# ScalarE takes over row statistics, the issue of two kinds of DMA, and a new order of the work

## The chip, the cores and the metric

The kernel runs on one core of a Trainium2 chip. A core has five engines, each with its own in-order stream of instructions: TensorE (PE, matrix multiply), VectorE (DVE), ScalarE (ACT), GpSimd (POOL) and SyncE (SP), which here does nothing but issue DMA transfers. They meet only through semaphores. An instruction that waits holds back everything behind it on its engine. The time is the device time of one execution, in microseconds (us). Before the change it was 1371.41 us, the median of three runs that lay between 1362.38 and 1377.51.

## The reference

Four transformer-like layers, A B A B, over 2048 tokens of width 512, with 32 heads of 16. Each layer normalizes its rows, projects to q, k and v, attends, projects back and adds to the residual. All of it is float32.

```python
x = x + _A_ref(_layernorm(x), A_wqkv, A_wo)
x = x + _B_ref(_layernorm(x), B_wqkv, B_wo)
x = x + _A_ref(_layernorm(x), A_wqkv, A_wo)
x = x + _B_ref(_layernorm(x), B_wqkv, B_wo)

def _layernorm(x, eps=1e-5):
    m, v = mean(x), var(x)              # over the 512 of a row
    return (x - m) / sqrt(v + eps)
# A: each token attends to itself and 7 earlier tokens, 2 apart
# B: each token attends to the 256 latest tokens, itself included
#    p = softmax(where(mask, q @ k.T * 16**-0.5, -1e9)); o = p @ v
```

## The kernel before, in words

**Tiling.** The tokens are cut into 8 chunks of 256. One B layer follows an A layer on the same chunks, so the work is a row of 32 scopes: A0, B0, A1, B1 and so on to A15, B15 (two passes over 8 chunks). All scopes overlap in time as far as their data and buffers allow.

**Precision.** Matmul operands that must be exact are split into a high float16 part and a low one (`xh`, `xl`; `eh`, `el`; `oh`, `ol`), and three products (high by high, high by low, low by high) are summed.

**Norm** (`norm`, L738). For each of the two halves of a chunk, DVE takes mean and variance (`stats`, L749 to L751), POOL makes the reciprocal standard deviation (`rstd`, L753 to L757), ACT writes the normalized rows (`xnorm`, L769) and their float16 high part (L781), SP issues a DMA that turns the high part (`turn_h`, L775), POOL or DVE subtracts (`rest`, L772) and SP issues the DMA that turns the low part (`turn_l`, L778). The projections on PE (L802 to L804 transposed, L823 plain) read the turned parts.

**Layer A.** ACT copies q, k, v out of PSUM (L936, L938). DVE or POOL forms the products of q with shifted k (`prod`, L960) and adds pairs (`plus`, L967); PE sums them to scores (L974); a softmax over 8 follows; DVE weighs v (L1046), and POOL or DVE adds up (`total`, L1051 to L1055).

**Layer B.** ACT writes the high part of q and k (`high`, L1074), DVE the low part (`low`, L1077). SP issues the writes of both to DRAM (`put`, L1087; twelve per scope, eight of them of high parts) and reads them back stacked along the rows (`stack`, L1098). A first pass of scores on PE (`tri`, `full`, L1130) gives DVE the row maxima (L1153, L1154, L1173); `mturn` (L1181 to L1184) joins and transposes them, ACT and POOL split them (L1187 to L1191), and SP sends them through DRAM (L1197) into the stacked operand (L1202). A second pass of scores (L1224) has the maxima subtracted by the matmul itself; ACT takes the exponentials (L1234), POOL masks them (L1245), PE multiplies with v (L1259). The score tiles `sc` have two buffers, so the DVE's reading of one frees it for PE's next.

**End of a layer** (`finish`, L833). The result is split, projected by `wo` (L823), and `done` (L867 to L869, DVE) adds it to the residual rows; SP stores them (L876, L880) and loads rows for the next norm (L843, L907).

**The order.** Nothing is scheduled while the program is built or run. Every step is a task with an engine and a cost in us, and a table `ORDER` gives, for each scope and each task in turn, its place on its engine. A negative entry means that the task goes to its other engine (DVE in place of POOL, or the reverse). `Plan.order` then walks through the queues and emits the instructions; costs only decide how the engines' streams are interleaved in the text of the program, and every engine's own order is that of the table.

```python
t.place, t.alt = ORDER[self.scope][self.k] if self.scope in ORDER else len(self.tasks), alt
if t.place < 0:
    (t.eng, t.us), t.place = alt, -1 - t.place
```

The functions that the change touches, and what calls them, with the line numbers of the profile:

Of the kernel before, what the change touches and what calls it, by code (L numbers as in the profile page):

```python
# [11 lines left out]
F32 = mybir.dt.float32  # L12
I32 = mybir.dt.int32
I16 = mybir.dt.int16
AF = mybir.ActivationFunctionType
# [26 lines left out]
        2, 3, 4, 4, 6, 6, 9, 4, 12, 8, 13, 11, 14, 13, 2, 1, 1, 0, 0, 3, 2, 7, 3, 33, 7, 5, 9, 7, 5, 10, 8, 11, 15, 17, 9, 25, 12, 18, 15, 17, 14,  # L42
        14, 15, 9, 12, 29, 20, 16, 45, 23, 32, 30, 34, 29, 36,
    ],
    "pB": [
        27, 43, 18, 44, 91, 89, 50, 95, 53, 49, 59, -75, 50, 66, -78, 17, 40, 25, 31, 84, 83, 46, 90, 49, 70, 45, 46, -60, 48, 51, 18, 26, 41, 20,
        27, 96, 97, 54, 100, 56, 55, 56, -62, 52, 53, -61, 6, 26, 15, 25, 54, 59, 31, 63, 35, 128, 37, 47, 35, 70, 86, 66, 19, 25, 36, 62, 1, 29, 31,
        28, 30,
    ],
# [4 lines left out]
    ],  # L54
# [5 lines left out]
    ],  # L60
# [8 lines left out]
    ],  # L69
# [5 lines left out]
    ],  # L75
# [10 lines left out]
    ],  # L86
# [5 lines left out]
    ],  # L92
# [1323 lines left out]
```

## Time and profile before

| what | us |
|---|---|
| median of three runs | 1371.41 |
| profiled execution | 1373.37 |
| its span, first to last instruction | 1371.6 |
| TensorE busy in it | 1246.9 |
| VectorE busy | 1142.3 |
| GpSimd busy | 955.4 |
| ScalarE busy | 733.7 |

The clock granted to TensorE was 0.973 of full speed on average. In the rows of the profile, `L802` is line 802 of the kernel, PEld is TensorE's loading of weights, and SPq or ACTq is the issue of a DMA by SP or ACT. A name such as `stk<-re` says that `stk` is written from `re`. Issuing a DMA is not counted as busy, although the engine does nothing else meanwhile. Busy times, waits and durations are those of the profiled execution.

### The profile page before, as it was taken

Reading aid. Unit: us, or ns where it says so; the run is one execution under the profiler, and the core shown is the slowest. Engines: PE = TensorE matmul, PEld = TensorE weight load, DVE = VectorE, ACT = ScalarE, POOL = GpSimd, SP = SyncE. Lnnn points to the kernel's source line nnn. Section 1 sums busy time; section 2 is a strip of 40 time slices with the busy share of each in tenths; the row PEclk is TensorE's granted clock in tenths of the full one; section 3 lists DMA queues with packets and bytes.
Section 4 is the critical chain, followed back from the end, with each engine's and each line's share of the span. In section 5 each row is a group of like instructions: output and inputs, shape, how many; then the busy total and the mean of one; then the engine's idle time right before and its main releaser. Section 6 shows DMA issues by size and latency. Waiting matters only on the chain.

```text
span 1371.6 us, 47863 instructions
## 1 busy us (share of the span) xinstructions
PE 1246.9 (91%) x20752; PEld 847.8 (62%) x20752; DVE 1142.3 (83%) x1482; ACT 733.7 (53%) x1035; POOL 955.4 (70%) x1013
## 2 busy tenths in 40 slices
PE   6869999989998898999999999998998999998877
PEld 4546666657566665666667666766666666664544
DVE  5968978887887888789899999798987988988574
ACT  7543454646555464655556464555555566365544
POOL 4357678778686877877686768888678877666233
PEclk9989999999999999999999999999999999999989
DMA  8204243334434332444434444433444434234322
GB/s 279 60 16 137 60 126 90 121 84 121 82 78 129 94 112 69 115 110 106 119 90 124 106 115 108 99 108 78 136 100 111 93 97 118 54 96 112 97 73 64
DMA packets 172467, 140.17 MB, mean 102 GB/s; under 512 B 105184, under 2 KB 131296, under 8 KB 172256
## 3 DMA queue, kind: packets, MB, share of 16 engines
q1 hardware_dynamic: 172000, 136.85, 38.1%
q8 instruction: 162, 2.65, 0.8%
q14 instruction: 49, 0.40, 0.1%
q10 hardware_dynamic: 256, 0.26, 0.1%
HBM read 67.11 MB, written 43.48 MB: 81 GB/s over the span
## 4 chain that ended last, share of the span: by engine, by line
PE 20%; DVE 12%; DMA 7%; SPq 4%; issue 3%; ACT 2%; POOL 2%; ACTq 0%; DVEq 0%; POOLq 0%
PE av L1259 3%; PE po L823 3%; PE pq L802 3%; PE pq L803 2%; PE pq L804 2%; DVE st L1153 2%; DVE m L1154 2%; DVE pw L1046 2%; DVE m L1173 2%; PE st L1130 2%; DMA xl<-xn 1%; DMA stk<-re 1%; SPq L1098 1%; DMA os<-scr 1%; SPq L1314 1%
## 5 line engine op out<-in xcount | busy, mean ns | idle before, releaser
L960 POOL TENSOR_TENSOR pr<-kv,q 128x1024 f32<-128x1024 f32 x76 | 170.5, 2253 | 41.9 <-DVE pr L967 16.2
L1153 DVE COPY_PREDICATED st<-maskt,st 128x512 f32<-128x512 int16 x224 | 154.0, 687 | 50.1 <-PE st L1130 46.1
L1234 ACT ACTIVATE p_H<-sk_H,scales 128x1024 f32<-128x1024 f32 x128 | 142.4, 1113 | 93.8 <-PE sk_H L1224 82.3
L1234 ACT ACTIVATE p_F<-sk_F,scales 128x1024 f32<-128x1024 f32 (+1 forms) x128 | 135.6, 1060 | 102.8 <-PE sk_F L1224 97.5
L1245 POOL TENSOR_SCALAR_AFFINE_SELECT p_H<-p_H 128x1024 f32<-128x1024 f32 x128 | 143.0, 1118 | 50.5 <-ACT p_H L1234 50.2
L1245 POOL TENSOR_SCALAR_AFFINE_SELECT p_L<-p_L 128x1024 f32<-128x1024 f32 x112 | 125.7, 1125 | 59.6 <-ACT p_L L1234 59.3
L1046 DVE TENSOR_TENSOR pw<-pb,kv 128x1024 f32<-128x1024 f32 x128 | 151.0, 1211 | 17.6 <-PE pb L1033 16.1
L1173 DVE TENSOR_REDUCE m<-sf 128x8 f32<-128x1024 f32 x120 | 144.8, 1211 | 22.8 <-PE sf L1130 22.5
L1154 DVE TENSOR_REDUCE m<-st 128x4 f32<-128x512 f32 x224 | 154.7, 691 | 7.7
L1234 ACT ACTIVATE p_L<-sk_L,scales 128x1024 f32<-128x1024 f32 x112 | 124.0, 1113 | 67.1 <-PE sk_L L1224 64.2
L1130 PEld LDWEIGHTS <-stk 48*128 48x128 f16 x2880 | 90.3, 95 | 109.3 <-issue 69.6
L1224 PEld LDWEIGHTS <-stk 64*128 64x128 f16 x2880 | 90.8, 95 | 100.8 <-issue 60.1
L1053 POOL TENSOR_TENSOR pw<-pw 128x512 f32<-128x512 f32 x87 | 110.9, 1274 | 28.8 <-DVE pw L1046 27.7
L1130 PE MATMUL st<-stk,stk 48*128 48x128 f16 x1920 | 97.4, 220 | 22.9 <-DMA stk<-re 8.0
L967 POOL TENSOR_TENSOR pr<-pr,pr 128x1024 f32<-128x1024 f32 x31 | 73.0, 2356 | 26.0 <-DVE pr L960 25.6
L1259 PE MATMUL av<-p_H,v 128*32 128x128 f32 x2048 | 81.1, 276 | 0.8 <-POOL p_H L1245 0.8
L1051 DVE TENSOR_REDUCE o<-pw 128x128 f32<-128x1024 f32 x41 | 79.9, 1953 | 0.2
L1259 PE MATMUL av<-p_F,v 128*32 128x128 f32 x1920 | 78.9, 280 | 0.7 <-ACT p_F L1234 0.6
L803 PE MATMUL pq<-xl,wA1h 128*128 128x256 f16 x256 | 70.7, 276 | 6.6 <-DMA xl<-xn 6.6
L960 DVE TENSOR_TENSOR pr<-kv,q 128x1024 f32<-128x1024 f32 x52 | 72.6, 1411 | 4.7 <-POOL pr L967 4.0
L803 PE MATMUL pq<-xl,wB1h 128*128 128x256 f16 x256 | 70.5, 275 | 6.5 <-DMA xl<-xn 6.3
L823 PEld LDWEIGHTS <-oh 128*32 128x32 f16 x2048 | 49.2, 98 | 43.5 <-issue 5.6
(194 smaller groups left out, 3592.7 us busy)
## 6 DMA issues: line engine op xcount, KB each, us to landing
stk<-re SPq DMA_DIRECT2D x256, 96.0 KB
re<-eh SPq DMA_DIRECT2D x128, 128.0 KB
xm<-xr SPq DMA_DIRECT2D x32, 256.0 KB
re<-el SPq DMA_DIRECT2D x64, 128.0 KB
xr<-xm SPq DMA_DIRECT2D x16, 512.0 KB
oc<-os SPq DMA_DIRECT2D x120, 64.0 KB
os<-scr SPq DMA_DIRECT2D x15, 512.0 KB
x<-in_A_x_dram SPq DMA_DIRECT2D x8, 512.0 KB
```

Of the source, the lines that this page charges most:

```text
L803: nc.tensor.matmul(ps[mp].t[:, i], wh, xl, start=False, stop=False)
L960: E.tensor_mul(pr.t, window(kv[1].t, m, P * n, P), qb)
L1046: nc.vector.tensor_mul(pw.t, pb.t.unsqueeze(1).broadcast_to([P, 2, W, 64]), v)
L1053: E.tensor_add(t[:, :, 0:4], t[:, :, 0:4], t[:, :, 4:8])
L1130: nc.tensor.matmul(ps.t[:, par, at * P : (at + 1) * P], stk[hf, 0][r, col, qb * P : (qb + 1) * P], stk[hf, kt][r, col, kb * P : (kb + 1) * ...
L1153: nc.vector.copy_predicated(v[:, :, 0::2], maskt[:, 0:P].bitcast(I16).unsqueeze(1).unsqueeze(1).broadcast_to([P, 2, 2, P]), v[:, :, 1::2])
L1154: nc.vector.tensor_reduce(out=m[:, 0, :, us[0]], in_=v[:, :, 0::2], op=ALU.max, axis=AX.X)
L1173: nc.vector.tensor_reduce(out=o, in_=v, op=ALU.max, axis=AX.X)
L1224: nc.tensor.matmul(ps.t[:, par, at * P : (at + 1) * P], stk[hf, kt][r, col, kb * P : (kb + 1) * P], stk[hf, 0][r, col, qb * P : (qb + 1) * ...
L1234: nc.scalar.activation(o, i, AF.Exp, scale=scl["B", 1])
L1245: nc.gpsimd.affine_select(out=v, in_=v, pattern=[[0, 8], [-1 if kind == "L" else 1, P]], compare_op=ALU.is_gt if kind == "L" else ALU.is_g ...
L1259: nc.tensor.matmul(acc.t[32 * mm : 32 * mm + 32, hq, qb * P : (qb + 1) * P], v[:, 17 * (H * kb + h) : 17 * (H * kb + h) + 32], p[:, mm % 2 ...
```

## The change

1. **Row statistics.** `stats` on the DVE is gone. ACT computes the variance of each half by a pass with Square, bias minus the mean and a sum over the row. In A layers ACT also computes the sum of the row by a pass with Copy; in B layers that sum comes from `done` of the A layer before, which now also returns the sum of each row that it writes.
2. **DMA issue.** `turn_h` and the writes of the high parts of q and k are issued by ACT in place of SP. The low parts stay on SP.
3. **Maxima.** `mturn` joins the two sets of maxima by a reduction that also doubles them, and transposes into the tile `mt`.
4. **Order.** `ORDER` is a new table for all scopes, prologue included, with other choices between DVE and POOL; some of the planner's costs change, and its cost for a change of matmul form goes from 0.15 to 0.17.

The diff, without the 550 lines of the table:

```diff
-TURN = 0.15
+TURN = 0.17
...
-        mv = buf("psm", [P, 2, 2], F32, "mv", f"mv{l}_{c}")
+        sums = layers[l] == "A"
+        if sums:
+            mv = buf("psm", [P, 2, 2], F32, "mv", f"mv{l}_{c}")
+            vsm = [Val(mv), Val(mv)]
+        else:
+            mv, vsm = x_sum[c]
...
-        def stats(t):
-            nc.vector.bn_stats(b6[t].t, xb.t[:, t])
-            nc.vector.bn_aggr(mv.t[:, t], b6[t].t)
+        xns = [buf("pxn", [P, D], F32, "xn", f"xn{l}_{c}_{t}") for t in range(2)]
+        vxq = [Val(x) for x in xns]
+
+        def rowsum(t):
+            nc.scalar.activation(xns[t].t, xb.t[:, t], AF.Copy, accum_out=mv.t[:, 0, t : t + 1])
+
+        def rowvar(t):
+            nc.scalar.activation(xns[t].t, xb.t[:, t], AF.Square, bias=mv.t[:, 0, t : t + 1], scale=-float(D), accum_out=mv.t[:, 1, t : t + 1])
...
         for t in range(2):
-            plan.add("DVE", 0.82, lambda t=t: stats(t), r=[vx[t]], w=[vmv[t], Val(b6[t])])
-        plan.add("POOL", 2.3, rstd, r=vmv, w=[vrs])
+            if sums:
+                plan.add("ACT", 0.72, lambda f=rowsum, t=t: f(t), r=[vx[t]], w=[vsm[t], vxq[t]])
+            plan.add("ACT", 0.72, lambda f=rowvar, t=t: f(t), r=[vx[t], vsm[t]], w=[vsq[t], vxq[t]])
+        plan.add("POOL", 1.95, rstd, r=vsq, w=[vrs])
...
             def turn_h(t=t, hi=hi):
-                nc.sync.dma_start_transpose(xh.t[:, :, t * P : (t + 1) * P], hi.t)
+                nc.scalar.dma_start_transpose(xh.t[:, :, t * P : (t + 1) * P], hi.t)
...
-            plan.add("SP", 1.26, turn_h, r=[vhi], w=[vh], size=10)
+            plan.add("ACT", 1.26, turn_h, r=[vhi], w=[vh], size=10)
...
-            def done(t=t, ps=ps):
+            def done(t=t, ps=ps, mv=x_sum[c][0] if T == "A" else None):
                 xt = xb.t[:, t]
-                nc.vector.scalar_tensor_tensor(xt, ps.t, scl[T, 3], xt, op0=ALU.mult, op1=ALU.add)
+                kw = {"accum_out": mv.t[:, 0, t : t + 1]} if mv else {}
+                nc.vector.scalar_tensor_tensor(xt, ps.t, scl[T, 3], xt, op0=ALU.mult, op1=ALU.add, **kw)
...
-                        nc.sync.dma_start(re.t[z, :, :, par].rearrange("q c u x -> (q c) u x"),
+                        (nc.scalar if n == "h" else nc.sync).dma_start(re.t[z, :, :, par].rearrange("q c u x -> (q c) u x"),
                                           e[n].t[:, par].rearrange("p i t -> p (i t)"))
 
-                    plan.add("SP", 0.59, put, r=ve[n], w=[vre[par][z]], size=128)
+                    plan.add("ACT" if n == "h" else "SP", 0.6, put, r=ve[n], w=[vre[par][z]], size=128)
...
-                a, b = (m[:, z, :, :, 1] if first else m[:, z].rearrange("p a u q -> p (a u q)") for z in range(2))
-                nc.vector.tensor_tensor(out=a, in0=a, in1=b, op=ALU.max)
-                nc.vector.transpose(mr.t, m.rearrange("p z a u q -> p (z a u q)"))
+                v = m.rearrange("p z a u q -> p (a u q) z")
+                o = mr.t.rearrange("p (r g) -> p r g", r=2)
+                if first:
+                    nc.vector.tensor_copy(o[:, :, 0::2], v[:, 0::2, 0].unsqueeze(1).broadcast_to([P, 2, 8]))
+                    o, v = o[:, :, 1::2], v[:, 1::2]
+                nc.vector.tensor_reduce(out=o, in_=v.unsqueeze(1).broadcast_to([P, 2, *v.shape[1:]]), op=ALU.max, axis=AX.X)
+                nc.vector.transpose(mt.t.bitcast(F32).rearrange("p a b -> p (a b)"), mr.t)
```

Left out beside the table: `rstd` rearranged for sums in place of mean and variance (the same four POOL instructions), the ACT and POOL steps behind `mturn` reading from the other tile, and the planner's smaller costs for six POOL steps.

More of the change, by code (lines that the diff above doesn't have):

```diff
@@ L733 @@
     x_in = {}
+    x_sum = {}
     x_mid = {}
@@ L740, in norm @@
         xb, vx = x_in[c]
-        mv = buf("psm", [P, 2, 2], F32, "mv", f"mv{l}_{c}")
+        sums = layers[l] == "A"
[4 more added lines that the diff above has]
+            mv, vsm = x_sum[c]
         rs = buf("psm", [P, 2, 2], F32, "rs", f"rs{l}_{c}")
-        b6 = [buf("ps1", [P, 6], F32, "b6", f"b6{l}_{c}_{t}") for t in range(2)]
-        vmv, vrs = [Val(mv), Val(mv)], Val(rs)
+        vsq, vrs = [Val(mv), Val(mv)], Val(rs)
         xh, xl = (buf("pxt", [P, 4, C], F16, n, f"{n}{l}_{c}") for n in ("xh", "xl"))
@@ L747, in norm @@
         d["vxt"] = []
-        def stats(t):
-            nc.vector.bn_stats(b6[t].t, xb.t[:, t])
-            nc.vector.bn_aggr(mv.t[:, t], b6[t].t)
+        xns = [buf("pxn", [P, D], F32, "xn", f"xn{l}_{c}_{t}") for t in range(2)]
[4 more added lines that the diff above has]
+            nc.scalar.activation(xns[t].t, xb.t[:, t], AF.Square, bias=mv.t[:, 0, t : t + 1], scale=-float(D), accum_out=mv.t[:, 1, t : t + 1])
         def rstd():
-            nc.gpsimd.tensor_scalar(rs.t[:, 0], mv.t[:, :, 1], 1.0e-5, 1.0 / (XS * XS), op0=ALU.add, op1=ALU.mult)
+            nc.gpsimd.tensor_scalar(rs.t[:, 0], mv.t[:, 1], 1.0 / (float(D) ** 3 * XS * XS), 1.0e-5 / (XS * XS), op0=ALU.mult, op1=ALU.add)
             nc.gpsimd.tensor_tensor(out=rs.t[:, 0], in0=rs.t[:, 0], in1=mhalf, op=ALU.pow)
             for t in range(2):
-                nc.gpsimd.tensor_scalar(rs.t[:, 1, t : t + 1], mv.t[:, t, 0:1], rs.t[:, 0, t : t + 1], -1.0, op0=ALU.mult, op1=ALU.mult)
+                nc.gpsimd.tensor_scalar(rs.t[:, 1, t : t + 1], mv.t[:, 0, t : t + 1], rs.t[:, 0, t : t + 1], -1.0 / D, op0=ALU.mult, op1=ALU.mult)
         for t in range(2):
-            plan.add("DVE", 0.82, lambda t=t: stats(t), r=[vx[t]], w=[vmv[t], Val(b6[t])])
-        plan.add("POOL", 2.3, rstd, r=vmv, w=[vrs])
+            if sums:
+                plan.add("ACT", 0.72, lambda f=rowsum, t=t: f(t), r=[vx[t]], w=[vsm[t], vxq[t]])
+            plan.add("ACT", 0.72, lambda f=rowvar, t=t: f(t), r=[vx[t], vsm[t]], w=[vsq[t], vxq[t]])
+        plan.add("POOL", 1.95, rstd, r=vsq, w=[vrs])
         for t in range(2):
-            xn = buf("pxn", [P, D], F32, "xn", f"xn{l}_{c}_{t}")
+            xn = xns[t]
             hi = buf("pxm", [P, D], F16, "xm", f"xm{l}_{c}_{t}")
-            vxn, vhi, vlo, vh, vl = Val(xn), Val(hi), Val(xn), Val(xh), Val(xl)
+            vxn, vhi, vlo, vh, vl = vxq[t], Val(hi), Val(xn), Val(xh), Val(xl)
             d["vxt"] += [vh, vl]
@@ L846, in finish @@
         x_in[c] = xb, vx
+        if T == "A":
+            mv = buf("ps1", [P, 2, 2], F32, "mvB", f"mv{l}_{c}")
+            x_sum[c] = mv, [Val(mv), Val(mv)]
         oh, ol = (buf("poh", [P, 4, C], F16, "o", f"o{z}{l}_{c}") for z in "hl")
@@ L865, in finish @@
             proj_n(T, 3, oh, ol, parts or [vh, vl], t, ps, vps)
-            def done(t=t, ps=ps):
+            def done(t=t, ps=ps, mv=x_sum[c][0] if T == "A" else None):
                 xt = xb.t[:, t]
-                nc.vector.scalar_tensor_tensor(xt, ps.t, scl[T, 3], xt, op0=ALU.mult, op1=ALU.add)
-            plan.add("DVE", 0.67, done, r=[vps, vscl[T, 3], vx[t]], w=[vx[t]])
+                kw = {"accum_out": mv.t[:, 0, t : t + 1]} if mv else {}
+                nc.vector.scalar_tensor_tensor(xt, ps.t, scl[T, 3], xt, op0=ALU.mult, op1=ALU.add, **kw)
+            plan.add("DVE", 0.78, done, r=[vps, vscl[T, 3], vx[t]], w=[vx[t], *([x_sum[c][1][t]] if T == "A" else [])])
             if T == "A":
@@ L928, in first @@
                     nc.gpsimd.tensor_copy(kv[s].t[:, :, :HALO], halo[l, c - 1, s][0].t)
-            plan.add("POOL", 0.5, first, r=[] if c == 0 else [halo[l, c - 1, s][1]], w=[vhalo[s]])
+            plan.add("POOL", 0.32, first, r=[] if c == 0 else [halo[l, c - 1, s][1]], w=[vhalo[s]])
         for s in range(3):
@@ L944, in layer_a @@
                 halo[l, c, s] = ha, vha
-                plan.add("POOL", 0.45, lambda s=s, ha=ha: nc.gpsimd.tensor_copy(ha.t, kv[s].t[:, :, C:]), r=vkv[s], w=[vha])
+                plan.add("POOL", 0.26, lambda s=s, ha=ha: nc.gpsimd.tensor_copy(ha.t, kv[s].t[:, :, C:]), r=vkv[s], w=[vha])
         L = buf("q_pj", [P, W, 64], F32, "pj", f"L{l}_{c}")
@@ L991, in clip @@
                                         compare_op=ALU.is_ge, fill=NEG, base=-HALO, channel_multiplier=0)
-            plan.add("POOL", 4.0, clip, r=[ve0], w=[ve1])
+            plan.add("POOL", 0.95, clip, r=[ve0], w=[ve1])
             src_, vsrc = e, ve1
@@ L1057, in layer_a @@
                 plan.add("DVE", 1.13, weigh, r=[vpb[th], *vkv[2], vhalo[2]], w=[vpw])
-                plan.add("POOL", 2.7, total, r=[vpw], w=[vr], alt=("DVE", 1.84))
+                plan.add("POOL", 2.58, total, r=[vpw], w=[vr], alt=("DVE", 1.84))
         finish(l, c, o, vo)
@@ L1179, in layer_b, with mturn @@
             vmr, vmt, vmd = Val(mr), [Val(mt), Val(mt)], Val(md)
-            def mturn(m=m, mr=mr):
-                a, b = (m[:, z, :, :, 1] if first else m[:, z].rearrange("p a u q -> p (a u q)") for z in range(2))
-                nc.vector.tensor_tensor(out=a, in0=a, in1=b, op=ALU.max)
-                nc.vector.transpose(mr.t, m.rearrange("p z a u q -> p (z a u q)"))
+            def mturn(m=m, mr=mr, mt=mt):
+                v = m.rearrange("p z a u q -> p (a u q) z")
[5 more added lines that the diff above has]
+                nc.vector.transpose(mt.t.bitcast(F32).rearrange("p a b -> p (a b)"), mr.t)
             def mhigh(mr=mr, mt=mt):
-                nc.scalar.activation(mr.t, mr.t, AF.Copy, scale=1.0 / MC)
+                nc.scalar.activation(mr.t, mt.t.bitcast(F32).rearrange("p a b -> p (a b)"), AF.Copy, scale=1.0 / MC)
                 nc.scalar.copy(mt.t[:, 0], mr.t)
@@ L1191, in mlow @@
                 nc.gpsimd.tensor_tensor(out=mt.t[:, 1], in0=mr.t, in1=mt.t[:, 0], op=ALU.subtract)
-            plan.add("DVE", 0.65, mturn, r=[vm], w=[vmr])
-            vms = Val(mr)
-            plan.add("ACT", 0.4, mhigh, r=[vmr], w=[vms, vmt[0]])
-            plan.add("POOL", 0.45, mlow, r=[vms, vmt[0]], w=[vmt[1]])
-            plan.add("SP", 0.59, lambda md=md, mt=mt: nc.sync.dma_start(md.t, mt.t), r=vmt, w=[vmd], size=30)
+            plan.add("DVE", 0.33, mturn, r=[vm], w=[vmr, vmt[0]])
+            vms, vml = Val(mr), Val(mt)
+            plan.add("ACT", 0.4, mhigh, r=[vmr], w=[vms, vmt[1]])
+            plan.add("POOL", 0.28, mlow, r=[vms, vmt[1]], w=[vml])
+            plan.add("SP", 0.59, lambda md=md, mt=mt: nc.sync.dma_start(md.t, mt.t), r=[vml], w=[vmd], size=30)
             for z in range(2):
```

10 lines of the change are left out of this document (5 added, 5 removed), and 463 rows, old and new, of the table ORDER.

## The prediction

> **What bounds the kernel now.** I read the page first, then the stretches of the span, then what TensorE waited for. The page's first lines set the floor:
>
> ```profile
> span 1371.6 us, 47863 instructions
> PE 1246.9 (91%) x20752; PEld 847.8 (62%) x20752; DVE 1142.3 (83%) x1482; ACT 733.7 (53%) x1035; POOL 955.4 (70%) x1013
> ```
>
> TensorE (PE) is busy for 1246.9 of 1371.6 us, so all its idle time is 124.7 us, and the change takes no matmul away. The table of stretches (length, then busy time of PE, PEld, DVE, ACT, POOL with counts, clock, DMA share, GB/s) says where that idle time lies:
>
> ```profile
> 0.00:34.00 34.00, 21.85 (x165) 16.71 (x165) 20.12 (x44) 24.60 (x37) 14.89 (x40) 1.00 0.90 278
> ...
> 420.00:560.00 140.00, 125.75 (x2254) 85.57 (x2244) 118.41 (x154) 74.37 (x102) 100.26 (x111) 0.99 0.40 109
> ...
> 700.00:840.00 140.00, 133.40 (x2224) 91.51 (x2223) 130.75 (x158) 75.65 (x115) 101.25 (x110) 1.00 0.42 113
> ...
> 1330.00:1372.00 42.00, 30.93 (x668) 17.83 (x664) 20.15 (x32) 19.95 (x23) 13.90 (x15) 0.92 0.25 72
> ```
>
> Start and end cost 12 and 11 us of PE. In the middle PE is busy for 125.75 (the worst stretch) to 133.40 (the best) of each 140 us, with the DVE close behind (118 and 131) and ScalarE (ACT) at little over half (74 and 76). So the middle can give back some 7 to 14 us in each 140, no more, and only where another engine or a queue makes PE wait. Who does that is in the list of PE's waits (total us, times, longest):
>
> ```profile
> PE pq L803 <- DMA xl<-xn: 12.9, 14, 2.8
> ...
> PE st L1130 <- DMA stk<-re: 8.0, 15, 1.1
> PE sk_H L1224 <- DMA stk<-md: 7.2, 4, 2.9
> PE st L1130 <- DVE m L1154: 4.8, 11, 0.8
> ...
> PE pq L802 <- DMA xh<-xm: 0.9, 1, 0.9
> ...
> PE av L1259 <- ACT p_F L1234: 0.6, 1, 0.6
> ...
> PE sk_L L1224 <- DVE m L1173: 0.6, 2, 0.3
> ```
>
> Two groups matter. Seven rows name a transfer that one of SP's instructions issues (turned activations, stacked q and k, row maxima), from 12.9 down to 0.9: 37.9 us in all. Ten rows name the DVE's maxima over the scores (L1154, L1173), which free the score tiles for PE, from 4.8 down to 0.6: 27.4 us. The change touches both.
>
> **What leaves the DVE.** The rows (count, then busy us, mean ns of one):
>
> ```profile
> L1183 DVE TENSOR_TENSOR m<-m 128x16 f32<-128x16 f32 (+1 forms) x64 | 33.2, 519 | 1.4
> ...
> L750 DVE BATCH_NORM_STATS2 b<-xr 128x6 f32<-128x512 f32 x32 | 22.1, 692 | 0.9
> L750 DVE BATCH_NORM_STATS2 b<-x 128x6 f32<-128x512 f32 x32 | 21.8, 681 | 5.6 <-DMA x<-in_A_x_dram 4.5 <-DMA x<-xd 0.8
> ...
> L751 DVE BATCH_NORM_AGGREGATE mv<-b 128x2 f32<-128x6 f32 x64 | 11.7, 182 | 2.2
> ```
>
> The row statistics go: 22.1 + 21.8 + 11.7 = 55.6 us. In `mturn` a maximum of 519 ns becomes a small reduction over 64 elements, which this trace does not show; its bounds are the 182 ns of the tiny aggregation and the 519 ns of what it replaces. I take 250, nearer the first, because it too reads one small tile: 64 x 0.27 = 17 us saved (0 to 22). The sum over the row that `done` now returns in the A layers is not in the trace either; I add one tiny instruction of 182 ns to each of 32, 6 us (bounds 0 and, at the 0.69 us of a whole further pass, 22).
>
> The negative entries of the new table move work between DVE and POOL: products (L960) on the DVE go from 52 to 60, pair sums (L967) from 33 to 40, and of the 512-element subtractions and scalings (`ol`, `rest`, `erest`, `omul`) two net come off the DVE, worth under 2 us.
>
> ```profile
> L960 POOL TENSOR_TENSOR pr<-kv,q 128x1024 f32<-128x1024 f32 x76 | 170.5, 2253 | 41.9 <-DVE pr L967 16.2 <-ACT q L936 13.8 <-ACT kv L938 7.5
> ...
> L967 POOL TENSOR_TENSOR pr<-pr,pr 128x1024 f32<-128x1024 f32 x31 | 73.0, 2356 | 26.0 <-DVE pr L960 25.6
> L960 DVE TENSOR_TENSOR pr<-kv,q 128x1024 f32<-128x1024 f32 x52 | 72.6, 1411 | 4.7 <-POOL pr L967 4.0 <-ACT q L936 0.6
> ...
> L967 DVE TENSOR_TENSOR pr<-pr,pr 128x1024 f32<-128x1024 f32 x33 | 42.7, 1296 | 1.3 <-POOL pr L960 0.9
> ```
>
> The DVE takes 8 x 1.41 + 7 x 1.30 = 20 us, POOL loses 8 x 2.25 + 7 x 2.36 = 35. Net the DVE falls by 55.6 + 17 - 6 - 20 + 2 = 49 us, to about 1093, from 88% to 84% in the middle. The DVE is not the end of the chain everywhere, so I let half of its 27.4 us go: **-14** (bounds 0 and -27). What is late next in those places is PE's own order.
>
> **What leaves SP and arrives on ACT.** Per layer and chunk two turnings (64 in all) and, in the 16 B chunks, eight writes of high parts (128). Their issues now (ns, min/median/max):
>
> ```profile
> L775 SPq DMA_TRANSPOSE xh<-xm x64: 1189/1257/2526, 12.1 to 1261.4; - x64
> L1087 SPq DMA_DIRECT2D re<-eh x128: 518/600/1482, 116.1 to 1283.3; - x128
> ```
>
> and SP's own waits:
>
> ```profile
> SPq L1087 <- ACT eh L1074: 60.2, 22, 8.7
> ...
> SPq L775 <- ACT xn L769: 35.3, 6, 20.6
> ```
>
> SP loses 64 x 1.257 + 128 x 0.600 = 157 us of issuing, and most of two waits in which everything behind stood still (60.2 and 35.3 us): stacking reads, maxima writes, gathers and the low parts' turnings. On ACT these waits vanish, because ACT itself makes the data. What a turning of low parts gains is seen at 865 us in the timeline, with the end of the flight from the chain of waits:
>
> ```profile
> 865.48 1.16 POOL L772 TENSOR_TENSOR xn<-xn,xm 128x512 f16<-128x512 f32 x1 [1.06 <-ACT xm L781]
> ...
> 865.50 1.96 SPq L775 DMA_TRANSPOSE xh<-xm  x1
> ...
> 867.55 2.56 SPq L778 DMA_TRANSPOSE xl<-xn  x2
> ```
>
> ```profile
> 868.86 4.22 DMA xl<-xn
> ```
>
> POOL had the last low part at 866.64, SP was busy with the high part to 867.46: 0.8 us is the gain there; the flight after it (4.22 us from the start of the second issue) stays. With 14 late ones that is 11 of the 12.9 us at best, and for the stacking and maxima, whose waits also hold flight, less. I take half of the 37.9: **-19** (bounds 0 and -38). Moving the high writes also frees `eh` sooner, which I leave at nothing: its cover is ACT's slack.
>
> ACT takes the 157 us and the statistics, 32 sums and 64 variances:
>
> ```profile
> L781 ACT CAST xm<-xn 128x512 f16<-128x512 f32 x64 | 39.0, 614 | 0.7
> ...
> L769 ACT ACTIVATE xn<-x,rs 128x512 f32<-128x512 f32 x32 | 25.5, 811 | 19.3 <-POOL rs L757 12.0 <-DMA xl<-xn 7.2
> ```
>
> ```profile
> L663 ACT ACTIVATION_READ_ACCUMULATOR wA1l<-stk x2: 185/186/187, 6.8 to 8.9; 128x1 f32 x2
> ```
>
> Without pointer operands an ACT pass over 512 elements is 614 ns, with two of them 811; the sum has none, the variance one (0.72 between them), and each is followed by a read of the accumulator of 186: 32 x 0.80 + 64 x 0.91 = 84 us. ACT goes from 734 to 818 us of busy time and, with issues, to 975, 71% of the span, some 73% in the middle. Queued behind each issue are mostly exponentials: in the new order the 192 issues stand in 100 groups, on average 1.57 us long and 2.5 at most, and 46 groups have an exponential right behind. What ACT has in hand is its wait for scores:
>
> ```profile
> ACT p_F L1234 <- PE sk_F L1224: 97.5, 64, 7.3
> ACT p_H L1234 <- PE sk_H L1224: 82.3, 56, 6.3
> ACT p_L L1234 <- PE sk_L L1224: 64.2, 53, 4.8
> ```
>
> 244 us in 173 waits, 1.4 us each, before 173 of 368 exponentials. So a group of 1.57 us is hidden about half the time; the other 50 delay an exponential by up to 1.57 us, 78 us if PE had nothing else to do. In the list above PE waits for p_F at L1259 0.6 us in all, so other work lies between scores and values now; I take a tenth: **+8** (bounds 0 and +78). The norm of an A chunk also becomes longer: two sums and two variances, 3.4 us on ACT against 2 x 0.87 on the DVE, 1.7 us x 16 = 27 if all were exposed. The nearest row is the 12.0 us that ACT now waits for `rs` ahead of the A norms (xn<-x above); I take a third of that: **+4** (bounds 0 and 27). In B the variance alone, 2 x 0.91, replaces 2 x 0.87: nothing.
>
> **The order of PE.** Counting changes of matmul form (whole array, column tiles, row tiles) in the two tables gives 957 before and 930 after. The first matmul after a change costs more in the chain:
>
> ```profile
> 910.88 0.22 PE pq L802
> ...
> 911.32 0.11 PE pq L802
> ```
>
> 27 x 0.11 = 3 us: **-3**. Other effects of the new order I cannot price; they are in the range.
>
> **The sum.** -14 - 19 + 8 + 4 - 3 = -24 us. The profiled execution took 1373.37 us, its span 1371.6; after: 1349.4 with a span of 1347.6. That execution lies 2.0 above the median of the runs shown, 1371.41, so I forecast a median of **1347**, 1.8% faster.
>
> **Rivals.** First, slower: **the two queues take turns.** Now all 128 turnings are issued by SP one behind the other. After it the high parts go from ACT, the low parts from SP. If a turning on one queue must wait until the other queue's has landed, each low part comes later by the flight, 4.22 - 1.25 = 3.0 us, and the gain in that wait is lost: 14 late norms x 3.0 + 6 = 48 us, 1395. If the emitted order alternates high, low, high, low, ACT itself stands for two flights less its own issue, 2 x 4.22 - 1.26 = 7.2 us, with exponentials behind it; in half of the 32 norms that is 115 us of ACT, and half of this on PE would bring 1450. The first form alone passes the 1% mark, 38 us above my forecast, when (38 - 6) / 3.0, some 11 of the 32 norms, are exposed so. For it: the two low issues follow the high one within 0.1 us at 867 us, so that in flight they overlap now. Against it: the diff writes no such wait. The Trainium skill, "DMA: Bandwidth & Descriptors", section "Silent corruption: two transposing streams in flight at once", says that transposes issued from SP and from ACT can corrupt each other when in flight together, so the later stream has to wait for the earlier one's full completion. No run shown here can confirm it, as one queue issues them all. Chance 0.17.
>
> Second, also slower: **ACT becomes the late engine.** If a third of the 78 us reaches PE and the norm's 27 us as well, the sum is -36 + 26 + 27 = +17: 1388. The table of stretches speaks against it, ACT being at 74 to 76 of 140 now. Chance 0.08.
>
> Third, no change: **the gain is eaten.** The waits on SP's transfers turn out to be flight, not issue (-5 in place of -19), and ACT's delays are +15: -14 - 5 + 15 + 4 - 3 = -3, 1368. For it: 4.22 us of flight against 0.8 of issue above. Chance 0.20.
>
> Fourth, more: both groups of waits vanish, -38 - 27 - 3 + 12 = -56: 1315. Chance 0.10.
>
> **Chances.** A measurement of this kernel tells 1% from no change, 1357.7 to 1385.1. My forecast (about 1325 to 1357) has 0.45, and with the fourth rival faster has 0.55; same 0.20; slower 0.25. The range 1318 to 1402 leaves out half of the fourth case and the worse half of the first. The forecast's own range is 1325 to 1357.
>
> **What would show it.** DVE busy near 1093 and no L750 rows; SP's waits on eh and xn nearly gone; ACT near 818 busy; PE's idle time near 100 with the rows of xl, stk and md halved. The first rival would show as low turnings, or ACT's high ones, waiting on transfers xh or xl, and larger PE waits on xl; the second as PE rows on p_F, p_H, p_L and rs above 30 us. A wrong forecast would most likely come from PE's new order, priced here only by its changes of form.

## The result, and the profile after

The changed kernel takes 1470.02 us (median of four runs, 1461.27 to 1473.92); the kernel before took 1368.64 beside it. The ratio that the runs give is 1.0768, with a 95% interval from 1.0721 to 1.0814 (the two medians are 101 us apart): slower by some 100 us, where 1347 had been forecast, and outside the forecast's range. The profiled execution lies below its median, with a span of 1459.5 us.

First the page of the changed kernel: span, busy time of each engine with its share of the span, and the chain of work that ended last.

```profile
span 1459.5 us, 47972 instructions
...
PE 1271.7 (87%) x20752; PEld 861.9 (59%) x20752; DVE 1092.2 (75%) x1407; ACT 794.5 (54%) x1227; POOL 918.2 (63%) x1000
...
PE 39%; DMA 16%; DVE 14%; ACT 9%; POOL 9%; issue 6%; SPq 4%; ACTq 3%; DVEq 0%; POOLq 0%
PE pq L819 7%; PE pq L820 6%; PE pq L821 6%; DMA xl<-xn 6%; PE av L1284 4%; DMA xh<-xm 4%; PE po L840 4%; DVE pw L1067 2%; DVE st L1174 2%; DVE m L1175 2%; PE st L1151 2%; PE pv L840 2%; ACTq L792 2%; DVE m L1194 2%; ACT p_H L1259 2%
```

The engines do what was foreseen: the DVE comes to 1092.2 us of work (forecast 1093), ACT to 794.5 (forecast 818). Yet PE, with the same 20752 matmuls, idles for 1459.5 - 1271.7 = 188 us in place of 125, and is itself busy for 25 us longer. In the chain stand the flights of turned activations (xl 6%, xh 4%) and `ACTq L792`, ACT's issue of the high parts' turning. (In the changed kernel the lines have moved: turnings of high and low parts are L792 and L795, projections L819 to L821, the exponentials L1259, the writes L1108.)

The table of stretches of the changed kernel (start:end and length; busy time of PE, PEld, DVE, ACT, POOL with counts; granted clock, DMA share, GB/s), for stretches shown of before, the worst one and the best:

```profile
0.00:34.00 34.00, 17.86 (x89) 11.27 (x90) 9.13 (x27) 24.46 (x45) 10.00 (x37) 1.00 0.64 201
...
280.00:420.00 140.00, 120.96 (x2049) 80.65 (x2048) 101.24 (x125) 71.22 (x106) 93.95 (x98) 0.93 0.37 92
420.00:560.00 140.00, 129.23 (x2219) 88.78 (x2220) 107.49 (x141) 83.33 (x134) 96.70 (x101) 0.98 0.37 96
...
700.00:840.00 140.00, 123.97 (x2072) 85.59 (x2075) 104.38 (x127) 79.75 (x123) 89.61 (x95) 0.93 0.38 95
...
1120.00:1260.00 140.00, 132.12 (x2276) 93.22 (x2280) 113.36 (x140) 86.79 (x128) 102.25 (x112) 0.96 0.39 100
```

The loss isn't in one place. In the middle PE used to be busy for 126 to 133 of each 140 us; now 121 is the worst stretch and 132 the best, and the granted clock is 0.93 to 0.98 there, in place of 0.96 to 1.00. DVE and POOL have less to do than before, and ACT is at 65 to 87 of 140: no other engine has become the bound.

PE's waits in the changed kernel (what it waited for: us in all, times, longest):

```profile
PE pq L819 <- DMA xh<-xm: 27.4, 12, 3.8
PE pq L820 <- DMA xl<-xn: 24.6, 11, 3.7
PE st L1151 <- ACT p_L L1259: 15.2, 4, 6.4
PE sk_L L1249 <- ACT p_H L1259: 10.4, 4, 4.4
...
PE sk_F L1249 <- ACT p_H L1259: 6.0, 4, 3.1
PE sk_L L1249 <- ACT p_L L1259: 5.3, 1, 5.3
```

Two groups have grown. Transfers that SP issued before (turned activations, stacked operands, maxima) cost PE 58.3 us over all rows, up from 37.9: the high parts rose from 0.9 to 27.4 and the low ones from 12.9 to 24.6, while stacked operands and maxima fell from 24.1 to 6.3. And rows that end with an exponential come to 49.3 us, up from 12.3, with single waits of up to 6.4 us, longer than any issue.

The exponentials and the low parts have one source; the row of the high parts stays where it is when the loss goes, as the experiments show. The two lines of turning in the changed kernel (ns of one: min/median/max; the semaphore instruction ahead of an issue is its wait; then who waited for it), high parts first:

```profile
L792 ACTq DMA_TRANSPOSE xh<-xm x64: 1205/1227/2446, 12.0 to 1360.3; - x64
L792 ACTq EVENT_SEMAPHORE  x48: 17/17/7255, 20.2 to 1353.8; - x48
```

```profile
  ACT p_L L1259: 26.2, 4
  PEld L820: 25.2, 10
  PE pq L820: 24.6, 11
  ACT xn L763: 14.5, 5
  ACT p_H L1259: 14.0, 2
```

The second fence is from the low parts' line, L795: ACT's exponentials waited 26.2 and 14.0 us for the turning of low parts. They don't read it. They stand behind a high turning on ACT, and that turning waits, up to 7.3 us, for a low turning from SP to land. The other direction is among SP's waits in the changed kernel, in a row that the kernel before doesn't have:

```profile
SPq L795 <- DMA xh<-xm: 111.8, 27, 8.2
```

In one place of the changed kernel both are seen in turn. The timeline (start, length, instruction, idle time before it and what ended it) at a norm near 865 us, the part of the span from which the prediction showed one:

```profile
864.45 2.53 ACTq L792 DMA_TRANSPOSE xh<-xm  x2
...
867.03 1.11 ACT L1259 ACTIVATE p_H<-sk_H,scales 128x1024 f32<-128x1024 f32 x1 [2.61 <-issue]
...
870.05 2.55 SPq L795 DMA_TRANSPOSE xl<-xn  x2
872.66 0.63 ACT L763 ACTIVATE xn<-x 128x512 f32<-128x512 f32 x1 [4.52 <-DMA xl<-xn]
...
873.91 0.39 PE L820 MATMUL pq<-xl,wB1h 128*128 128x256 f16 x1 [3.66 <-DMA xl<-xn]
```

Before, SP issued the low pair 0.1 us behind the high pair. Now the low pair leaves at 870.05, 3.1 us after the last high issue had ended, although the last subtraction of POOL that makes its data (not shown) had ended at 865.66. PE waits 3.66 us for it. ACT's next statistics pass waits 4.52 us as well, because it writes into the tile that the low turning reads.

### The profile page after: what moved, and what is told of

The parts are those of the page before. It is cut to its first block, busy times and chain, and to the rows that moved or that the text cites. A ratio compares the mean times of both kernels' runs of the same rounds, so it can differ in the third digit from the quotient of the medians.

```text
span 1459.5 us, 47972 instructions
## 1 busy us (share of the span) xinstructions
PE 1271.7 (87%) x20752; PEld 861.9 (59%) x20752; DVE 1092.2 (75%) x1407; ACT 794.5 (54%) x1227; POOL 918.2 (63%) x1000
## 4 chain that ended last, share of the span: by engine, by line
PE 39%; DMA 16%; DVE 14%; ACT 9%; POOL 9%; issue 6%; SPq 4%; ACTq 3%; DVEq 0%; POOLq 0%
PE pq L819 7%; PE pq L820 6%; PE pq L821 6%; DMA xl<-xn 6%; PE av L1284 4%; DMA xh<-xm 4%; PE po L840 4%; DVE pw L1067 2%; DVE st L1174 2%; DVE m L1175 2%; PE st L1151 2%; PE pv L840 2%; ACTq L792 2%; DVE m L1194 2%; ACT p_H L1259 2%
## 5 line engine op out<-in xcount | busy, mean ns | idle before, releaser
L1259 ACT ACTIVATE p_H<-sk_H,scales 128x1024 f32<-128x1024 f32 x128 | 141.8, 1112 | 112.1 <-PE sk_H L1249 52.8
L1259 ACT ACTIVATE p_F<-sk_F,scales 128x1024 f32<-128x1024 f32 (+1 forms) x128 | 135.5, 1059 | 90.5 <-PE sk_F L1249 73.2
L981 POOL TENSOR_TENSOR pr<-kv,q 128x1024 f32<-128x1024 f32 x68 | 151.5, 2236 | 19.0 <-DVE pr L988 13.2
L1259 ACT ACTIVATE p_L<-sk_L,scales 128x1024 f32<-128x1024 f32 x112 | 124.3, 1113 | 70.2 <-PE sk_L L1249 43.8
L1151 PE MATMUL st<-stk,stk 48*128 48x128 f16 x1920 | 94.4, 220 | 26.8 <-ACT p_L L1259 15.2
L819 PE MATMUL pq<-xh,wB1h 128*128 128x256 f16 x256 | 81.5, 318 | 22.3 <-DMA xh<-xm 19.7
L1098 DVE SCALAR_TENSOR_TENSOR el<-pq,eh 128x512 f16<-128x512 f32 x64 | 42.6, 686 | 72.4 <-ACT eh L1095 71.0
L820 PE MATMUL pq<-xl,wB1h 128*128 128x256 f16 x256 | 81.7, 319 | 16.9 <-DMA xl<-xn 16.9
L981 DVE TENSOR_TENSOR pr<-kv,q 128x1024 f32<-128x1024 f32 x60 | 87.5, 1470 | 4.3 <-POOL pr L988 2.9
L821 PE MATMUL pq<-xh,wB1l 128*128 128x256 f16 x256 | 81.1, 317 | 0.0
L820 PE MATMUL pq<-xl,wA1h 128*128 128x256 f16 x256 | 73.7, 288 | 7.8 <-DMA xl<-xn 7.8
```

Of the source, the lines that this page charges most:

```text
L819: nc.tensor.matmul(ps[mp].t[:, i], wh, xh, start=k == 0, stop=False)
L820: nc.tensor.matmul(ps[mp].t[:, i], wh, xl, start=False, stop=False)
L821: nc.tensor.matmul(ps[mp].t[:, i], wl, xh, start=False, stop=k == 3)
L981: E.tensor_mul(pr.t, window(kv[1].t, m, P * n, P), qb)
L1151: nc.tensor.matmul(ps.t[:, par, at * P : (at + 1) * P], stk[hf, 0][r, col, qb * P : (qb + 1) * P], stk[hf, kt][r, col, kb * P : (kb + 1) * ...
L1259: nc.scalar.activation(o, i, AF.Exp, scale=scl["B", 1])
```

## The experiments

Two theories stood against each other at first. **Queues take turns**: turnings issued from different queues are never in flight together, each change of queue costs a flight, and the engine that holds the later issue stands still. **ACT's load**: 192 issues and 96 passes on ACT hold up the exponentials, whatever they are. As the first was borne out, a third question was left, what the new **order** and the statistics do by themselves. All ratios are to the kernel before on the same chip, with 95% intervals. An edit of an issue changes only the engine that issues: the program is written in the same order, and the moved instruction stands at the same place of it.

### The one word alone, and its undoing

In the kernel before, high turnings go to ACT and nothing else:

```diff
-                nc.sync.dma_start_transpose(xh.t[:, :, t * P : (t + 1) * P], hi.t)
+                nc.scalar.dma_start_transpose(xh.t[:, :, t * P : (t + 1) * P], hi.t)
```

> The kernel before, with one word changed: ScalarE issues the turning of the high parts, at the same places of the program (old order, statistics on the VectorE, writes on SP). Two queues that take turns: 60 to 110 us slower than before, 1430 to 1480, with SP waiting for transfer xh ahead of low turnings. ScalarE too late: 80 us more issuing on an engine with idle time, at most +40, 1410. The new order: same as before, 1370.

Measured: 1501.18 us, ratio 1.0971 (1.0913 to 1.1029). The one word costs more than the whole change. The chain of waits of this kernel shows the turns, one after the other (start, length, what):

```profile
617.67 4.11 DMA xh<-xm
...
621.84 1.25 SPq L778
...
623.14 3.24 DMA xl<-xn
...
626.53 1.21 ACTq L775
...
628.39 1.01 ACT p_H L1234
```

The high part lands, SP issues two low ones, they land, ACT issues the next high one, and behind it a copy and an exponential of other data get their turn. PE's waits show that this hits the exponentials more than the projections: rows that end with an exponential rose from 12.3 to 70.2 us over all rows (those that end with any work of ACT from 31.2 to 123.9), while the row of xl is nearly where it was (12.9 before):

```profile
PE st L1130 <- ACT p_F L1234: 20.0, 7, 5.2
...
PE pq L803 <- DMA xl<-xn: 14.2, 8, 3.1
PE sk_L L1224 <- ACT p_H L1234: 10.9, 4, 6.1
PE sk_F L1224 <- ACT p_L L1234: 9.5, 5, 4.4
```

The reverse, the changed kernel with that word undone:

> The changed kernel, but SP issues the turning of the high parts again, at the same places of the program; all else (statistics and writes on ScalarE, new order) stays. Two queues that take turns: no turning waits for the other queue any more, so most of the 100 us comes back, 1365 to 1390 us, and SP's waits for transfer xh ahead of its low turnings fall from 111.8 us to below 20. ScalarE too late: half of what it issues (80 of 157 us) is gone, half of the loss comes back, about 1420. The new order: little changes, above 1440.

Measured: 1401.73 us, ratio 1.0226 (1.0172 to 1.0281), 68 us faster than the changed kernel, and SP's row of 111.8 us is gone. It reaches neither what was expected nor the kernel before: SP now issues high turnings at places planned for ACT, and PE waits longest for them:

```profile
PE pq L819 <- DMA xh<-xm: 46.8, 20, 5.0
```

### Half the dose

Only the high turnings of the B norms (32) go to ACT:

```diff
+                (nc.scalar if layers[l] == "B" else nc.sync).dma_start_transpose(xh.t[:, :, t * P : (t + 1) * P], hi.t)
```

> The kernel before with half of the one-word edit: only the high turnings of the B norms (32) go to ACT. With all 64 on ACT the time went up by 133 us. If each change from one queue to the other has its price, some half of that is seen: 1420 to 1445. If the loss comes from a few places alone (the A norms, whose turnings the projections need at once), it is small, under 1385, or nearly whole, over 1480.

Measured: 1430.62 us, ratio 1.0461 (1.0429 to 1.0494): half. In the written order of the 128 turnings the queue changes 73 times with all high ones on ACT and 40 times here. 0.0971 and 0.0461 of 1368 us are 133 and 63 us: 1.8 and 1.6 us for each change.

### The same number of issues on ACT, without the turns

Now 64 turnings go to ACT by layer: both parts of the A norms, while the B norms stay on SP. The queue changes only between norms, 29 times.

```diff
+                (nc.scalar if layers[l] == "A" else nc.sync).dma_start_transpose(xh.t[:, :, t * P : (t + 1) * P], hi.t)
...
+                (nc.scalar if layers[l] == "A" else nc.sync).dma_start_transpose(xl.t[:, :, t * P : (t + 1) * P], xn.t.bitcast(F16)[:, 0:D])
```

> The kernel before, in which ScalarE issues all turnings (high and low) of the A norms and SP all of the B norms: 64 turnings on ScalarE as in the run with the high parts alone, but the queue changes only between norms, not within one. Two queues that take turns: the waits are mostly over before they matter, 1370 to 1400 us. The issue load on ScalarE: as slow as with the high parts alone, near 1500.

Measured: 1364.16 us, ratio 0.998 (0.9954 to 1.0006): nothing lost. The same edit in the changed kernel:

> The changed kernel with one edit: turnings go to ACT by layer (all of the A norms), not by part (all high ones); 64 are on ACT as in the changed kernel. If the queues' turns are the cause of the loss, nearly all of the 100 us goes: 1365 to 1385, near the 1376 of the changed kernel with all turnings on ACT. If the load of 64 turnings on ACT or the new statistics are the cause, it stays near 1470. If the new order, made for high turnings on ACT and low ones on SP, is what costs the rest, it stays above the 1366 of the kernel before.

Measured: 1377.69 us, ratio 1.0071 (1.0048 to 1.0095). 92 us of the loss are gone, with 64 turnings, 128 writes and 96 statistics passes still on ACT. The wait ahead of ACT's high turnings is gone too; this is the line that showed 7255 ns at most in the changed kernel:

```profile
L792 ACTq EVENT_SEMAPHORE  x7: 17/17/17, 18.0 to 917.4; - x7
```

Of PE's waits, those that end with an exponential fall from 49.3 to 17.6 us, and those for low parts from 24.6 to 3.4. The row of the high parts stays, so the turns are not what it comes from:

```profile
PE pq L819 <- DMA xh<-xm: 27.3, 16, 4.5
...
PE pq L820 <- DMA xl<-xn: 3.4, 6, 1.0
```

The span is 88 us shorter (1371.3 for 1459.5): 59 of them are idle time of PE and 29 busy time (1242.3 for 1271.7).

Finally all 128 turnings on ACT, one queue again, first in the kernel before, then in the changed one:

> The kernel before, in which ScalarE issues all 128 turnings, 160 us of issuing, and SP none. Two queues that take turns: no change of queue, so no such wait; 1365 to 1395 us. ScalarE too late: twice the load of the run with the high parts alone, 1500 us or more.

> The changed kernel, with the low turnings issued by ScalarE too, so that all 128 turnings are on one queue again, and ScalarE issues 80 us more. Two queues that take turns: no waits between turnings of different queues, but ScalarE now waits for the low parts from the VectorE and GpSimd: 1380 to 1430 us, below the changed kernel. ScalarE too late: more load and more waiting on it, 1500 us or more. The new order: no forecast.

Measured: 1374.41 us, ratio 1.0051 (1.0025 to 1.0077), and 1375.69 us, ratio 1.0068 (1.0031 to 1.0104). Twice as many turnings on ACT cost 7 us in the old order. With all of them on one queue, the line of semaphores in the changed kernel is short as well:

```profile
L792 ACTq EVENT_SEMAPHORE  x23: 17/17/17, 18.6 to 1277.7; - x23
```

ACT's load isn't the cause; the turns are.

### The writes

The writes of the high parts alone, in the kernel before; and their return to SP in the changed one:

```diff
-                        nc.sync.dma_start(re.t[z, :, :, par].rearrange("q c u x -> (q c) u x"),
+                        (nc.scalar if n == "h" else nc.sync).dma_start(re.t[z, :, :, par].rearrange("q c u x -> (q c) u x"),
```

> The kernel before, in which ScalarE issues the writes of q's and k's high parts, at the same places of the program; all turnings stay on SP. Two queues that take turns: writes do not wait for each other across queues, so what was forecast of them holds, 1350 to 1370 us (SP has 77 us less to issue). ScalarE too late: 1375 to 1395.

> The changed kernel, but SP issues the writes of q's and k's high parts again; the high turnings stay on ScalarE. Two queues that take turns: the waits of the turnings stay, 1445 to 1480 us. ScalarE too late: 77 of its 157 us of issuing are gone, about 1420. The new order: above 1440.

Measured: 1352.38 us, ratio 0.9883 (0.9833 to 0.9933), and 1486.39 us, ratio 1.0867 (1.0826 to 1.0908), 16 us above the changed kernel (14 by the ratios). So this part of the change is a gain of about 15 us in both settings, and **the kernel before with it alone is faster than both kernels**. Of the 21 us by which the profiled span is shorter, 11 are idle time of PE and 10 busy time (1236.6 for 1246.9). In the idle time it is the rows of SP's transfers that fell; these answer to 12.9, 8.0 and 7.2 before:

```profile
PE pq L803 <- DMA xl<-xn: 9.0, 12, 1.3
...
PE st L1130 <- DMA stk<-re: 4.2, 8, 1.5
PE sk_H L1224 <- DMA stk<-md: 4.1, 5, 1.7
```

SP itself doesn't stand less. Its wait for the high parts, 60.2 us before, is gone, but at the writes of the low parts it now waits for the DVE (2.3 us before):

```profile
SPq L1087 <- DVE el L1077: 74.5, 23, 7.8
```

So the gain is shown, and that SP's transfers come sooner; that it comes from less waiting on SP is not.

Can more be had? The same with turnings by layer, and then with the writes of the low parts on ACT as well:

> The kernel before with two edits at once: the 128 writes of high parts are issued by ACT, and of the turnings those of the A norms (64, high and low) by ACT, those of the B norms by SP. ACT gets the same 192 issues as in the changed kernel, in another split. If the loss of the changed kernel comes from the two queues taking turns, the edits add up: 0.988 x 0.998 of the time before, about 1350 us (1340 to 1358). If it comes from 192 issues on ACT, whatever they are, the loss shows again: 1400 or more. If the moved writes gain because SP stands less behind turnings, half of that gain is had already by moving turnings, and the two together give no more than the writes alone, 1352.

> The kernel before with the writes of high and low parts (128 and 64) on ACT, all turnings on SP. With the high ones alone 1352. If SP's in-order waits for eh and el are what the writes cost, the wait for el (the next largest on SP) goes too, 1340 to 1350. If ACT, which doesn't make the low parts, now stands waiting for the DVE with exponentials behind it, 1352 to 1375.

Measured: 1356.39 us, ratio 0.9915 (0.9888 to 0.9942), and 1362.13 us, ratio 0.9945 (0.9919 to 0.9971). Neither beats the high writes alone. In the last one ACT waits for the writes of low parts to give the tiles back, 16.7 us where it was 3.0 with the high writes alone (and 13.4 in the kernel before, so that this row alone doesn't explain the difference):

```profile
ACT eh L1074 <- DMA re<-el: 16.7, 3, 7.2
```

### Statistics and order

The first kernel with the high writes on ACT and turnings by layer (1356) and the changed kernel with turnings by layer (1378) issue the same transfers from the same engines. Between them lie the statistics, the joining of maxima and the order: +22 us, where the forecast had -13. First the order with the rest undone (turnings and writes on SP, statistics on the DVE, the old joining):

> The changed kernel's new order with everything else undone: statistics on DVE (their places are those of the new passes on ACT, so the DVE does them in the order in which the program is written), all turnings and writes issued by SP, the old joining of maxima. If the order by itself is neutral, some 1366 to 1375 us. If the order costs what the sum lacks (the changed kernel with all turnings on ACT takes 1376, where the writes' gain of 14, the statistics' of 19 and a cost of 8 for the turnings leave 1341), then 1390 to 1430, with part of it owed to SP, which has to issue high turnings at places meant for ACT.

Measured: 1425.45 us, ratio 1.0445 (1.0408 to 1.0482). Much of that need not be the order as such: it was made for other engines. PE's waits for turned, stacked and maxima transfers come to 78.3 us over all rows, since SP again has everything. So this run gives only an upper bound.

The changed kernel with all turnings on ACT, and its statistics back on the DVE:

> The changed kernel with all turnings on ScalarE, and in addition mean and variance on the VectorE again, at the same places of the program (VectorE about 50 us more, ScalarE about 80 us less, and done gives no row sums). Against the run with all turnings on ScalarE alone (1376): if the statistics on ScalarE cost what was forecast (4 us for the longer norm and a part of the 8), 1365 to 1375; if the relief of the VectorE was worth the 14 us forecast, 1380 to 1390.

Measured: 1394.71 us, ratio 1.0198 (1.0145 to 1.0251), 19 us slower than with the statistics on ACT. In this order the DVE's relief is worth having; but the DVE does the statistics here at places found for ACT, so 19, too, is no clean price.

The cleaner cut leaves the statistics out. In the changed kernel with turnings by layer, each pass is cut to one element:

```diff
-            nc.scalar.activation(xns[t].t, xb.t[:, t], AF.Copy, accum_out=mv.t[:, 0, t : t + 1])
+            nc.scalar.activation(mv.t[:, 0, t : t + 1], xb.t[:, t, 0:1], AF.Copy)
...
-            nc.scalar.activation(xns[t].t, xb.t[:, t], AF.Square, bias=mv.t[:, 0, t : t + 1], scale=-float(D), accum_out=mv.t[:, 1, t : t + 1])
+            nc.scalar.activation(mv.t[:, 1, t : t + 1], xb.t[:, t, 0:1], AF.Copy, bias=float(D) ** 3, scale=0.0)
```

> The changed kernel with turnings split by layer (1378 us), in which each of the 96 statistics passes on ACT is cut to a copy of one element straight into the statistics tile. It leaves out the computation of mean and variance (the variance is a constant), for the time alone; the tile of normalized rows isn't written by these passes any more, so they don't wait for the turning of the norm before. If the 22 us that separate it from the kernel before with the same split of issues (1356) are the statistics on ACT, their length and their wait together, it comes to 1350 to 1360. If they are the new order, it stays at 1370 or more.

In the other version the one element still goes into `xns[t]`, with the accumulator, so that the wait for that tile stays:

> As the kernel with the passes cut, but the one element is written into the tile of normalized rows, as the whole pass does, so that the wait for that tile stays and only the length of the passes goes. Mean and variance are left out here too. If the length of the passes on ACT costs, it lies with the other cut kernel (within 4 us). If the wait for the tile costs, it lies nearer the uncut 1378, 8 us or more above the other.

Measured: 1371.32 us, ratio 1.0003 (0.997 to 1.0036), and 1374.61 us, ratio 1.0026 (0.9991 to 1.0061). By ratios, 0.0068 of 1368 us: the statistics passes on ACT cost 9 us (beyond the one element that is left of each), and 0.0023, 3 us, of it may be the wait for the tile, which the intervals don't tell from nothing. That leaves 0.0088, 12 us, to the order (with the new joining), even with the DVE relieved and ACT free of most of the passes. What it consists of is partly visible in the PE waits of the first cut kernel:

```profile
PE pq L819 <- DMA xh<-xm: 25.7, 15, 3.3
```

With the old order and the same split this row is 0.8 us. The B norms' high turnings are on SP here, at places made for ACT, so part of the 12 us may be owed to this split and not to the order. With all turnings on ACT and the statistics whole the row is 13.8, but PE waits more for exponentials (39.6 us over all rows, against 17.6 with the split by layer), and the time is the same. Which order these statistics would want was not tried, nor were the statistics on ACT in the old order.

## Why the prediction was wrong

The loss can be laid out from the kernel before to the changed one by the runs, each step by its difference of ratios times 1368 us:

| step | us | forecast |
|---|---|---|
| high writes to ACT | -16 | in -19 and +8 |
| half of the turnings to ACT, by layer | +4 | in -19 and +8 |
| new order, joining, statistics off the DVE, passes on ACT cut to one element | +12 | -14, -3 |
| statistics passes on ACT whole | +9 | +4 |
| turnings split by part instead of by layer | +95 | 0 (rival, chance 0.17) |

The steps add up to the 105 us of the ratio 1.0768 because each starts where the last one ended. Each single ratio is known to 0.3 to 0.5%, 4 to 7 us, so a step is known to some 6 to 8 us: the +4 can't be told from nothing, the +9 and +12 only just, and the +95 stands far outside this.

**The step that failed** is that the sum has no term for the wait between the two queues. It was left to the rivals, where it was played down: "Against it: the diff writes no such wait." The diff writes none, and the program has them all the same: the semaphore ahead of ACT's high turnings is there in the trace, 17 ns long where ACT issues all and up to 7255 ns where two queues take turns. In the programs as built, 64 of the changed kernel's 128 turnings have ahead of them a wait for a turning from the other queue; with all turnings on one queue, or split by layer, none has. The rival's own sign came true, low turnings that wait for xh (111.8 us). That sentence made 0.17 of a mechanism that was in the program, and it cost 95 us. The page named in that rival, "DMA: Bandwidth & Descriptors" of the Trainium skill, section "Silent corruption: two transposing streams in flight at once", asks that the later stream wait for the full completion of the earlier one; the trace agrees with the wait (a low pair issued 3.1 us after the last high issue, not 0.1). What happens to the data without it, no run here shows.

**Its price** was too low as well. The block form, 1395, counted only PE's wait for low parts. In the changed kernel the turns put 21 us on this wait (24.6, against 3.4 with the split by layer); in the one-word edit it hardly moved (12.9 to 14.2 us). The second form, ACT standing for a flight with exponentials behind it, weighs more: 12.3 to 70.2 us of PE's waits in the one-word edit, and 49.3 in the changed kernel against 17.6 with the split by layer. That PE's busy time would grow as well, by 25 us, no rival had. Per turn the price was too high, 3.0 us where the runs give 1.4 to 1.8 for each change of queue; but it was put on 14 late norms, and the written order changes between high and low 93 times among 128 turnings. The sketch of 1450, with half of the norms alternating, was the nearer one, and 1470 is still 20 above it.

**The other terms.** "What leaves the DVE", 49 us of work, was right to about a microsecond (50.1), and in the passes on ACT the estimates of 0.80 and 0.91 us met 0.82 and 0.90 (625 + 191 and 716 + 189 ns). ACT's busy time grew by 61 us and not by the 84 of these rows, as some of them overlap with others in time. The -14 made of the DVE's relief isn't confirmed: between the two kernels with turnings by layer PE's waits for the DVE's maxima fell only from 26.7 to 21.4 us over all rows. "What leaves SP", -19, had nearly the right size for the writes alone (-16), and PE's waits for SP's transfers did fall; but of the two reasons given, less issuing and less standing, the second failed, as SP stands for the low parts instead (74.5 us). The moving of turnings brought no time, not even by layer (0.998), although PE's wait for low parts halved there, from 12.9 to 6.2 us: SP's lateness with them was not what the time hung on. "+8" for ACT's issues was in place: 7 us with 128 turnings on ACT. "+4" for the statistics measured 9. "The order of PE", -3 by changes of form, said nothing about the order; the warning at the end of the prediction, that the order would be the likeliest way to be wrong, named 12 us at most, not the 95.

## What to carry to other kernels

Before moving one of two kinds of DMA to another queue, look for what the two kinds share: the turnings from two queues were made to take turns here, and the wait stands on the issuing engine with all its other work behind it. Split such transfers by phase, so that one norm's turnings stay on one queue, and alternate as seldom as possible. Move what its own producer makes, alone and unmixed: the plain writes of the high parts were the one part of this change that paid by itself in the kernel before, by 1.2%, and a change with many parts is worth trying part by part.

## What the runs showed of the hardware

**The granted clock follows the waiting.** In the changed kernel PE needed 25 us more for the same matmuls. The row of one group of them in the list of groups (busy us, mean ns of one) has 318 ns, where its counterpart, the first row, had 276 before. The group stands right behind PE's waits for turned parts; one that doesn't, the last row, keeps its time (274 ns before):

```profile
L802 PE MATMUL pq<-xh,wB1h 128*128 128x256 f16 x256 | 70.6, 276 | 1.0 <-DMA xh<-xm 0.9
```

```profile
L819 PE MATMUL pq<-xh,wB1h 128*128 128x256 f16 x256 | 81.5, 318 | 22.3 <-DMA xh<-xm 19.7 <-ACT xn L763 2.6
...
L819 PE MATMUL pq<-xh,wA2h 128*128 128x256 f16 x256 | 71.1, 278 | 0.1
```

One such place is the norm near 865 us, where PE waits 3.66 us up to 873.91. The table of stretches, asked for before, just behind and some time behind this wait (the clock is the third number from the end), has the clock at half behind it:

```profile
866.00:870.00 4.00, 2.63 (x48) 1.79 (x46) 4.00 (x5) 1.11 (x1) 1.80 (x1) 1.00 0.89 155
874.00:877.00 3.00, 3.00 (x15) 2.13 (x16) 0.98 (x1) 2.73 (x8) 2.60 (x4) 0.50 0.04 5
878.00:882.00 4.00, 4.00 (x45) 3.43 (x45) 0.86 (x2) 1.77 (x3) 0.50 (x2) 1.00 0.00 0
```

A matmul of this group takes 0.42 us at 874.30 and 0.27 us at 879.04.

Over the whole span the clock was 0.973 before and 0.952 after; 0.973 / 0.952 = 1.022, and busy time grew by 1271.7 / 1246.9 = 1.020. With the one word alone it was 0.939 and PE busy 1280.1; with the high writes alone 0.981 and 1236.6. So a quarter to a third of the loss (25 of 88 us of span) is the price of having waited. The sum of idle time isn't all that matters: the order alone idled for 1421.5 - 1254.7 = 167 us and kept 0.971. How long a wait must be to cost the clock was not measured. "TensorE: Matmul & The Clock Gate" of the Trainium skill, Part 1, has the array throttled by default and released by activity; the trace agrees in direction.

**Two queues in turn cost a flight for each change.** Pieces of the chain of the changed kernel (start, length, what), where high and low parts alternate:

```profile
473.82 2.46 DMA xl<-xn
476.30 3.93 DMA xh<-xm
...
480.28 2.44 DMA xl<-xn
...
482.80 1.45 ACTq L792
```

Here the low turnings land 2.4 to 2.5 us after the start of their issue and the high one after 3.9, and the next one from the other queue starts less than 0.1 us later each time (482.80 is ACT's issue, 480.28 + 2.44 = 482.72 the landing before it). Why the high one took longer is not shown; the DMA engines were busier meanwhile, a mean share of 0.76 against 0.32 and 0.34 in the flights of the low ones. One queue sends the next turning after 1.25 us, the length of an issue, two queues only after the flight: 1.2 us more for each change with the shorter flight, 2.7 with the longer. The 1.4 us that separate the changed kernel from its split by layer (92 us over 93 - 29 = 64 changes) and the 1.6 to 1.8 of the one-word edits lie between. How much of them is flight, and how much the clock and the work queued behind, no run of its own shows.
